# Softmax reciprocals repeated through DRAM, value products copied out by ScalarE and scaled later by GpSimd

## The chip, the cores and the metric

The kernel runs on one core of a Trainium2 chip. The metric is the device time of one execution in microseconds (us), lower being better. The core has five engines that run their own instruction queues and wait for one another by semaphores: TensorE (PE in the profile; its weight loads are shown as PEld), VectorE (DVE), ScalarE (ACT), GpSimd (POOL) and SyncE (SP), which here only issues DMA transfers. TensorE writes its results into PSUM, the other engines work on PSUM and SBUF.

## The reference

Causal attention with a decay, for 4 batches of 8 heads, 576 positions and 64 columns a head, and behind it two feed-forward layers (512 to 2048 to 512) over the 2304 tokens. What the change touches is the last step of the attention:

```python
scores = scores - np.max(scores, axis=-1, keepdims=True)
attn = np.exp(scores)
attn = attn / (np.sum(attn, axis=-1, keepdims=True) + 1e-09)
return np.matmul(attn, v).astype(np.float32)
...
h = x @ w_in                       # first layer; x is the attention's output
g = h * np.clip(h + 3.0, 0.0, 6.0) / 6.0
x = g @ w_out
h = x @ w_in2                      # second layer
return (np.maximum(h, 0.0) + alpha * np.minimum(h, 0.0)) @ w_out2
```

The kernel doesn't divide the scores' exponentials; it multiplies by the values first and scales the product by the reciprocal of the row's sum.

## The kernel before

Attention works on 16 pairs of heads (4 batches of 4 pairs). A pair is cut into nine units: four blocks of 128 query rows of the first head (positions 0 to 3), the last 64 rows of both heads together (position 4), four blocks of the second head (positions 5 to 8). One loop counts units, and in each step the instructions of several units are written in an order fixed by the string ORD = "TMEVDS": T transposes the exponentials of the unit five steps back (L396, L400, TensorE), M takes row maxima of the unit one step back (L340, VectorE), E does the exponentials of the unit two steps back (L348, ScalarE, with the row sums), V copies the transposed tile out of PSUM (L407, L412 and L413; ScalarE, every fourth block VectorE), D runs the steps that were put off to this time, S does the scores of the step's own unit (L363 to L380, TensorE). No scheduler reorders them: each engine runs its instructions in this order.

The steps put off belong to a pair whose last unit is U. At U + 3 (RD) `recips` forms ten reciprocals a row on VectorE and has GpSimd repeat them 64 times into rw (L93, called at L425). At U + 6 (SD) `spread` has TensorE transpose rw (four transposes tr at L435, one tj at L438), and ScalarE copies the result into rcb: one reciprocal for each column of the output, repeated over the 64 partitions of a head (L436, L440 twice). At U + 7 (PA) and U + 9 (PB) `stage3` forms the value products of output columns 0 to 255 and 256 to 575 (L453), both in the one PSUM buffer pv, and VectorE multiplies pv by rcb into the token array R (L460). U + 6 is position 5 of the next pair, U + 7 position 6, U + 9 position 8. Below, the two products are called the first and the second product of a pair; pairs are counted from 0.

R holds the tokens in three blocks of 768, so that the 576 tokens of batches 1 and 2 lie over a border (`x_places`), and their pieces are cut there.

In the same steps the heads of the next pair are prepared: `prep_head` (positions 3 and 7; GpSimd, L93 for q and k), two steps later `prep_low` (L331 on GpSimd, L332 on VectorE) and `copy_k` (a DMA from SBUF to SBUF, L325). SyncE issues all of these transfers in the order of the program: the head's rows (L295 rqk), the values (L300), the constant rows (L312, L313), copy_k. Conversions of the feed-forward weights and of the first tokens are laid between units by tables (CONV_ATT and others; lines 138 to 187 and 240 to 248), on ScalarE, VectorE and GpSimd.

Buffers: three PSUM buffers of tag tp, which the transposes of the exponentials share with tr and tj; one buffer for pv; four for the scores; one for rcb.

From position 147 on the steps of the feed-forward layers begin (DRAIN), and behind the attention they run alone to the end.

Of the kernel before, what the change touches and what calls it, by code (L numbers as in the profile page):

```python
# [21 lines left out]
def decay_attention_ffn2_kernel(ctx, tc, qk, v, f, wi1, wo1, wi2, wo2, alpha, out):  # L22
# [20 lines left out]
    LM, LE, LT, LV = 1, 2, 5, 5  # L43
    RD, SD, PA, PB = 3, 6, 7, 9
    DRAIN = {9 * NP + 3: 2, 9 * NP + 4: 2, 9 * NP + 6: 2, 9 * NP + 7: 2}
# [36 lines left out]

    f_d = [dram.tile([128, 4, KH * 256], F32, name=f"fd{g}") for g in range(NC)]
    aq_d = dram.tile([2, 32, 4, QW], F32, name="aq_d")
    ak_d = dram.tile([2, 32, 4, S], F32, name="ak_d")
# [192 lines left out]
    def attention():  # L278
        with ExitStack() as ax:
# [135 lines left out]
            def recips(p):  # L415

                ss = sm.pop(p)
                rc = st.tile([128, 10], F32, tag="rc", name="rc")
                nc.vector.tensor_scalar(out=ss[:, 4:5], in0=ss[:, 4:5], scalar1=ss[:, 9:10], scalar2=None,
                                        op0=ALU.add)  # L420
                nc.vector.tensor_copy(out=ss[:, 9:10], in_=ss[:, 4:5])
                nc.vector.tensor_scalar(out=rc, in0=ss, scalar1=1e-9, scalar2=None, op0=ALU.add)
                nc.vector.reciprocal(out=rc, in_=rc)
                rw = rcp.tile([128, KT, 2, 64], F32, tag="rw", name="rw")
                scaled(  # L425
                    "P", rw, rc.rearrange("p (a i) -> p i a", a=2).unsqueeze(3).broadcast_to([128, KT, 2, 64]))
                rcs[p] = rw

            def spread(p):

                rw = rcs.pop(p)
                t = rcp.tile([128, S], F32, tag="rcb", name="rcb")
                tr = ps_pt.tile([128, 4, 128], F32, tag="tp", name="tr")
                for i in range(4):
                    nc.tensor.transpose(tr[:, i, :], rw[:, i].rearrange("p a b -> p (a b)"), ident)  # L435
                nc.scalar.copy(out=t[:, 0:512], in_=tr.rearrange("p a b -> p (a b)"))  # L436
                tj = ps_pt.tile([128, 4, 128], F32, tag="tp", name="tj")
                nc.tensor.transpose(tj[:, 0, :], rw[:, 4].rearrange("p a b -> p (a b)"), ident)  # L438
                for a in range(2):
                    nc.scalar.copy(out=t[64 * a:64 * a + 64, 512:S], in_=tj[64 * a:64 * a + 64, 0, 64 * a:64 * a + 64])  # L440
                rcb[p] = t

            def stage3(p, part):
# [5 lines left out]
                for j in js:  # L449
                    lo = max(q0, 128 * j)  # L450
                    kk = min(128, S - 128 * j)
                    for a in range(2):
# [3 lines left out]
                            rhs=pts[2 * p + a][0:kk, j * PR + lo:j * PR + q1],  # L456
                            start=(j == js[0]), stop=(j == js[-1]))
                for view, t0, t1 in x_places(hp, b * S + q0, b * S + q1):
                    c0, c1 = t0 - b * S, t1 - b * S
                    nc.vector.tensor_mul(out=view, in0=pv[:, c0 - q0:c1 - q0], in1=rcb[p][:, c0:c1])  # L460
                if part == 1:
                    for d, key in ((vs, p), (rcb, p), (pts, 2 * p), (pts, 2 * p + 1)):
                        d.pop(key)

# [97 lines left out]
            for k, (a, h) in enumerate(zip(("", "l0", "l1", "l2", "a3", "a4", "a6", "l3", "l4", "a5", "l6", "l5"),  # L562
                                           ("0", "1", "2", "", "", "", "3", "4", "6", "", "5", ""))):
                for c in range(KH):
                    if a:
                        aside(places[k], {"l": lows, "a": adds}[a[0]][int(a[1]), c])
                    if h:
                        aside(places[k], highs[int(h), c])
            for t in range(len(units) + max(LV, PB) + 1):
                now = todo.pop(t, [])  # L570
# [12 lines left out]
                if t < len(units):  # L583
                    p, ab, i = units[t]
                    pos = t % 9
                    if ab == 1 and i == 3:
                        for d, fn in ((RD, lambda p=p: recips(p)), (SD, lambda p=p: spread(p)),
                                      (PA, lambda p=p: stage3(p, 0)), (PB, lambda p=p: stage3(p, 1))):
                            todo.setdefault(t + d, []).append(fn)
# [324 lines left out]
```

## Time and profile before

| | us |
|---|---|
| median of 3 runs (982.57 to 983.43) | 982.98 |
| the profiled execution | 982.49 |
| its span | 980.7 |
| TensorE busy | 955.6 (97%) |
| VectorE busy | 705.7 (72%) |
| GpSimd busy | 594.4 (61%) |
| ScalarE busy | 539.7 (55%) |

The profiled execution lies 0.49 us under the median and 1.79 us over its own span. Busy shares are averages over two stages with different limits: attention, about 0 to 222 us, and the layers behind it, in which TensorE is busy in nearly every slice. In the timelines a row's length is that of one instruction from its start to its end, and neighbours overlap a little, so the distance from one start to the next is shorter than a length.

### The profile page before, as it was taken

How to read it: one execution, taken by the hardware profiler on the slowest of the kernel's cores; microseconds unless marked ns; L12 is line 12 of the kernel's file. 1: busy time of each engine (PE TensorE's matmuls, PEld its weight loads, DVE VectorE, ACT ScalarE, POOL GpSimd, SP SyncE). 2: the span in 40 equal slices, each digit the busy share in tenths (PEclk: the TensorE clock that was granted, in tenths of full speed). 3: DMA queues.
4: the chain of work that ended last, by engine and by line, in shares of the span. 5: the costliest groups of instructions: out<-in, count | busy, mean ns of one | idle time of the engine just before them, and what ended most of it. 6: DMA issues, size and time to landing. Idle time of an engine off the chain costs nothing.

```text
span 980.7 us, 15789 instructions
## 1 busy us (share of the span) xinstructions
PE 955.6 (97%) x5488; PEld 860.4 (88%) x5488; DVE 705.7 (72%) x1274; ACT 539.7 (55%) x1348; POOL 594.4 (61%) x583
## 2 busy tenths in 40 slices
PE   5999999999999999999999999999999999999998
PEld 4767766678999999999999999899898988898897
DVE  7898979956697777876788666347897778625454
ACT  5678877777555554555564456644454546343231
POOL 7567589956646665578476379565646668422231
PEclk9999999999999999999999999999999999999999
DMA  7646576501414443410468732413434410253541
GB/s 211 201 136 213 181 250 196 144 35 43 161 65 182 183 183 108 160 59 9 166 246 312 272 130 108 161 65 140 173 118 182 182 65 17 103 204 139 216 161 64
DMA packets 36195, 145.79 MB, mean 149 GB/s; under 512 B 4860, under 2 KB 4860, under 8 KB 33012
## 3 DMA queue, kind: packets, MB, share of 16 engines
q1 hardware_dynamic: 36112, 144.79, 42.0%
q8 instruction: 43, 0.70, 0.3%
q14 instruction: 36, 0.29, 0.1%
q10 hardware_dynamic: 4, 0.00, 0.0%
HBM read 97.21 MB, written 43.42 MB: 143 GB/s over the span
## 4 chain that ended last, share of the span: by engine, by line
PE 85%; DVE 8%; issue 2%; POOL 2%; ACT 1%; SPq 1%; DMA 1%; POOLq 0%; DVEq 0%; ACTq 0%
PE o L744 20%; PE hA L704 20%; PE o L742 19%; PE hC L704 10%; PE hB L704 5%; PE pv L453 4%; DVE nm L340 2%; PE tp L396 2%; PE sc L363 2%; DVE q L332 1%; PE sc L364 1%; DVE pt L407 1%; POOL g L687 1%; DMA k<-ak_d 1%; PE sc L375 0%
## 5 line engine op out<-in xcount | busy, mean ns | idle before, releaser
L687 POOL TENSOR_TENSOR g<-t,g 128x384 fp32r<-128x384 f32 x192 | 205.6, 1071 | 287.6 <-ACT g L686 270.4
L742 PE MATMUL o<-g,wo 128*128 128x384 f32 x1152 | 232.2, 340 | 1.8 <-POOL wo L187 1.1
L704 PE MATMUL hA<-xh,wi 128*128 128x384 f32 x768 | 224.3, 338 | 1.1 <-DVE hD L718 0.7
L744 PE MATMUL o<-wo,g 128*128 128x512 f32 x864 | 223.2, 394 | 0.0
L742 PEld LDWEIGHTS o<-g,wo 128*128 128x128 f32 x1152 | 205.0, 189 | 3.2 <-POOL wo L187 1.4
L686 ACT CAST g<-t 128x384 fp32r<-128x384 f32 x192 | 98.6, 514 | 176.8 <-DVE t L681 91.8
L744 PEld LDWEIGHTS o<-wo,g 128*128 128x128 f32 x864 | 160.6, 188 | 25.8
L762 DVE TENSOR_TENSOR r<-o,r 128x512 f32<-128x512 f32 x126 | 86.7, 688 | 86.2 <-PE o L744 85.7
L704 PEld LDWEIGHTS hA<-xh,wi 128*128 128x128 f32 x768 | 141.5, 188 | 4.7 <-DVE hD L718 1.0
L704 PE MATMUL hA<-xl,wi 128*128 128x384 f32 x384 | 129.5, 337 | 0.0
L751 DVE SCALAR_TENSOR_TENSOR r<-o,r 128x384 f32<-128x384 f32 x168 | 92.1, 552 | 49.1 <-PE o L742 48.3
L704 PE MATMUL hC<-xh,wi 128*128 128x384 f32 x384 | 114.4, 338 | 0.0
L348 ACT ACTIVATE p<-sc,nm 128x128 f32<-128x128 f32 (+4 forms) x160 | 84.2, 530 | 16.6 <-DVE nm L340 14.5
L340 DVE TENSOR_REDUCE nm<-sc 128x1 f32<-128x128 f32 (+4 forms) x160 | 71.6, 469 | 6.1 <-PE sc L365 4.0
L704 PEld LDWEIGHTS hA<-xl,wi 128*128 128x128 f32 x384 | 72.1, 188 | 3.2
L704 PEld LDWEIGHTS hC<-xh,wi 128*128 128x128 f32 x384 | 71.3, 189 | 2.1 <-issue 0.2
L248 POOL TENSOR_TENSOR xl<-r,xh 128x384 fp32r<-128x384 f32 x59 | 69.7, 1197 | 3.3 <-ACT xh L243 2.8
L396 PE MATMUL tp<-ident,p 128*128 128x128 f32 x384 | 68.6, 282 | 1.0 <-ACT pt L412 0.6
L363 PE MATMUL sc<-k,q 128*128 128x256 f32 (+2 forms) x128 | 55.0, 429 | 12.2 <-DVE k L331 8.8
L709 ACT COPY s<-hA 128x384 f32<-128x384 f32 x96 | 45.8, 477 | 35.1 <-PE hA L704 34.9
L704 PE MATMUL hC<-xl,wi 128*128 128x384 f32 x192 | 65.0, 338 | 0.0
L704 PE MATMUL hB<-xh,wi 128*128 128x384 f32 x192 | 57.1, 338 | 0.0
(133 smaller groups left out, 1725.6 us busy)
## 6 DMA issues: line engine op xcount, KB each, us to landing
wid<-wi SPq DMA_DIRECT2D x24, 896.0 KB
wi<-wid SPq DMA_DIRECT2D x12, 1792.0 KB
rqk<-in_qk SPq DMA_DIRECT2D x32, 608.0 KB
raw<-in_wi SPq DMA_DIRECT2D x32, 512.0 KB
raw<-in_wo SPq DMA_DIRECT2D x32, 512.0 KB
wod<-wo SPq DMA_DIRECT2D x24, 512.0 KB
wo<-wod SPq DMA_DIRECT2D x12, 1024.0 KB
vt<-in_v SPq DMA_DIRECT2D x16, 320.0 KB
```

The costliest lines, as they stand in the source:

```text
L248: e.tensor_sub(out=XS[k][1][:, b, c], in0=x, in1=XS[k][0][:, b, c].bitcast(F32))
L340: nc.vector.tensor_reduce(out=nm[:, i:i + 1], in_=src, axis=AX.X, op=ALU.max, negate=True)
L348: nc.scalar.activation(out=pt[:, c0:c0 + cw], in_=src, func=AF.Exp, bias=nm[:, 0:1], scale=1.0, accum_out=dsts[i])
L363: nc.tensor.matmul(out=sc[:, 0:n], lhsT=q1[:, qs], rhs=k1[:, 0:n], start=True, stop=False)
L396: nc.tensor.transpose(tp[:, j, :], pt[:, 128 * j:128 * j + 128], ident)
L686: nc.scalar.copy(out=gt[n][i][:, 0], in_=hold["g"])
L687: nc.gpsimd.tensor_sub(out=gt[n][i][:, 1], in0=hold["g"], in1=gt[n][i][:, 0].bitcast(F32))
L704: nc.tensor.matmul(out=h, lhsT=a, rhs=b[:, x, kc], start=new and kc + e == 0, stop=kc == KH - 1 and e == 2, skip_group_check=not new)
L742: nc.tensor.matmul(out=o[:, 0:NB], lhsT=a[:, cs], rhs=b, start=st, stop=sp)
L744: nc.tensor.matmul(out=o, lhsT=b[:, cs], rhs=a, start=st, stop=sp)
L751: later(0, lambda: nc.vector.scalar_tensor_tensor(out=acc, in0=o[:, 0:NB], scalar=1.0 / 6.0, in1=acc, op0=ALU.mult, op1=ALU.add))
L762: nc.vector.tensor_add(out=acc, in0=o, in1=acc)
```

## The change

`recips` no longer has GpSimd repeat the reciprocals. `spread` transposes the 128 x 10 tile rc once; ScalarE copies the 10 x 128 result to SBUF, and SyncE stores it in DRAM (rc_d). `widen`, two steps later (U + 8), has SyncE read it back in three transfers that repeat a row over 64 partitions, into rcb. `stage3` only forms the products. `settle`, one step behind each product (U + 8 and U + 10), has ScalarE copy pv into R unscaled, and `normalize` (U + 12, PN) has GpSimd multiply R in place by rcb.

```diff
--- before.py
+++ after.py
@@ -41,7 +41,7 @@
     TAIL = S - 512
     PR = S - 128
     LM, LE, LT, LV = 1, 2, 5, 5
-    RD, SD, PA, PB = 3, 6, 7, 9
+    RD, SD, PA, PB, PN = 3, 6, 7, 9, 12
     DRAIN = {9 * NP + 3: 2, 9 * NP + 4: 2, 9 * NP + 6: 2, 9 * NP + 7: 2}
     CONV_ATT = "m0 22 f0 23 s0 24 j0 25 g0 26 m1 31 f1 32 s1 33 j1 34 g1 35 hb 37 lb 39 S1 42 S3 42 S2 45 S4 45 ha 51 la 54 hc 53 lc 60 hd 60 ld 63 m2 69 f2 70 s2 71 j2 72 g2 73 m3 78 f3 79 s3 80 j3 81 g3 83 ho0 78 lo0 87 ho1 87 lo1 91 wi0 90 wi1 93 wo0 99 wo1 102 r0 54 r1 63 r2 93 r3 104"
     CONV_ATT1 = "r0 131 r1 141 m0 108 f0 109 s0 110 j0 114 g0 115 m1 117 f1 118 s1 119 j1 123 g1 124 S1 143 S3 145 S2 146 ha 146 hc 146 hb 147 la 147 lc 147 lb 148 S4 149 hd 149 ld 150 m2 150 f2 151 s2 151 j2 152 g2 153"
@@ -81,6 +81,7 @@
     wo_d = [[dram.tile([128, 2, FT * DM], F32, name=f"wod{ff}{g}") for g in range(NG)] for ff in range(2)]
 
     f_d = [dram.tile([128, 4, KH * 256], F32, name=f"fd{g}") for g in range(NC)]
+    rc_d = [dram.tile([2, KT * 128], F32, name=f"rc{i}") for i in range(NP)]
     aq_d = dram.tile([2, 32, 4, QW], F32, name="aq_d")
     ak_d = dram.tile([2, 32, 4, S], F32, name="ak_d")
 
@@ -421,24 +422,31 @@
                 nc.vector.tensor_copy(out=ss[:, 9:10], in_=ss[:, 4:5])
                 nc.vector.tensor_scalar(out=rc, in0=ss, scalar1=1e-9, scalar2=None, op0=ALU.add)
                 nc.vector.reciprocal(out=rc, in_=rc)
-                rw = rcp.tile([128, KT, 2, 64], F32, tag="rw", name="rw")
-                scaled(
-                    "P", rw, rc.rearrange("p (a i) -> p i a", a=2).unsqueeze(3).broadcast_to([128, KT, 2, 64]))
-                rcs[p] = rw
+                rcs[p] = rc
 
             def spread(p):
 
-                rw = rcs.pop(p)
+                rc = rcs.pop(p)
+                tr = ps_pt.tile([128, 4, 128], F32, tag="tp", name="tr")
+                nc.tensor.transpose(tr[0:2 * KT, 0, :], rc, ident)
+                flat = rcp.tile([2 * KT, 128], F32, tag="rw", name="rw")
+                nc.scalar.copy(out=flat, in_=tr[0:2 * KT, 0, :])
+                nc.sync.dma_start(out=rc_d[p].rearrange("a (i c) -> (a i) c", c=128), in_=flat)
+
+            def widen(p):
+
                 t = rcp.tile([128, S], F32, tag="rcb", name="rcb")
-                tr = ps_pt.tile([128, 4, 128], F32, tag="tp", name="tr")
-                for i in range(4):
-                    nc.tensor.transpose(tr[:, i, :], rw[:, i].rearrange("p a b -> p (a b)"), ident)
-                nc.scalar.copy(out=t[:, 0:512], in_=tr.rearrange("p a b -> p (a b)"))
-                tj = ps_pt.tile([128, 4, 128], F32, tag="tp", name="tj")
-                nc.tensor.transpose(tj[:, 0, :], rw[:, 4].rearrange("p a b -> p (a b)"), ident)
-                for a in range(2):
-                    nc.scalar.copy(out=t[64 * a:64 * a + 64, 512:S], in_=tj[64 * a:64 * a + 64, 0, 64 * a:64 * a + 64])
+                for a, c0, w in ((0, 0, S), (1, 0, 512), (1, 512, TAIL)):
+                    s0 = c0 + TAIL * (c0 > 0)
+                    nc.sync.dma_start(out=t[64 * a:64 * a + 64, c0:c0 + w],
+                                      in_=rc_d[p][a, s0:s0 + w].unsqueeze(0).broadcast_to([64, w]))
                 rcb[p] = t
+
+            def normalize(p):
+                b, hp = divmod(p, NPAIR)
+                t = rcb.pop(p)
+                for view, t0, t1 in x_places(hp, b * S, b * S + S):
+                    nc.gpsimd.tensor_mul(out=view, in0=view, in1=t[:, t0 - b * S:t1 - b * S])
 
             def stage3(p, part):
                 b, hp = divmod(p, NPAIR)
@@ -455,12 +463,18 @@
                             lhsT=vt[0:kk, j, 64 * a:64 * a + 64],
                             rhs=pts[2 * p + a][0:kk, j * PR + lo:j * PR + q1],
                             start=(j == js[0]), stop=(j == js[-1]))
+                if part == 1:
+                    for d, key in ((vs, p), (pts, 2 * p), (pts, 2 * p + 1)):
+                        d.pop(key)
+                pvs[p, part] = pv
+
+            def settle(p, part):
+                b, hp = divmod(p, NPAIR)
+                pv = pvs.pop((p, part))
+                q0, q1 = ((0, 256), (256, S))[part]
                 for view, t0, t1 in x_places(hp, b * S + q0, b * S + q1):
-                    c0, c1 = t0 - b * S, t1 - b * S
-                    nc.vector.tensor_mul(out=view, in0=pv[:, c0 - q0:c1 - q0], in1=rcb[p][:, c0:c1])
-                if part == 1:
-                    for d, key in ((vs, p), (rcb, p), (pts, 2 * p), (pts, 2 * p + 1)):
-                        d.pop(key)
+                    c0, c1 = t0 - b * S - q0, t1 - b * S - q0
+                    nc.scalar.copy(out=view, in_=pv[:, c0:c1])
 
 
             NPP = 64
@@ -566,7 +580,8 @@
                         aside(places[k], {"l": lows, "a": adds}[a[0]][int(a[1]), c])
                     if h:
                         aside(places[k], highs[int(h), c])
-            for t in range(len(units) + max(LV, PB) + 1):
+            pvs = {}
+            for t in range(len(units) + max(LV, PN) + 1):
                 now = todo.pop(t, [])
                 for ch in ORD:
                     if ch == "D":
@@ -585,7 +600,9 @@
                     pos = t % 9
                     if ab == 1 and i == 3:
                         for d, fn in ((RD, lambda p=p: recips(p)), (SD, lambda p=p: spread(p)),
-                                      (PA, lambda p=p: stage3(p, 0)), (PB, lambda p=p: stage3(p, 1))):
+                                      (PA, lambda p=p: stage3(p, 0)), (PA + 1, lambda p=p: settle(p, 0)),
+                                      (SD + 2, lambda p=p: widen(p)), (PB, lambda p=p: stage3(p, 1)),
+                                      (PB + 1, lambda p=p: settle(p, 1)), (PN, lambda p=p: normalize(p))):
                             todo.setdefault(t + d, []).append(fn)
                     if pos == 2:
                         load_v(p)
```

Three places show how the queues change; L numbers are those of each kernel.

ScalarE, before: the stretch between the copies into rcb of a pair (L436, L440) and the exponentials that follow the second copy of three transposed blocks (L407 with 128x3x128).

```order
L436 COPY rcb<-tr 128x512 [waits PE_49]
L440 COPY rcb<-tj 64x64 [waits PE_49]
L440 COPY rcb<-tj 64x64
L348 ACTIVATE p,sm<-sc,nm 128x288 [waits DVE_49,Activation_49]
L348 ACTIVATE p,sm<-sc,nm 128x288
L407 COPY pt<-tp 128x2x128 [waits PE_49]
L138 ACTIVATE wc<-raw 128x512 [waits DMAHW0_49,Pool_49]
L348 ACTIVATE p,sm<-sc,nm 128x128 [waits DVE_49,Activation_49]
L407 COPY pt<-tp 128x3x128 [waits PE_49]
L348 ACTIVATE p,sm<-sc,nm 128x256 [waits DVE_49,Activation_49]
L348 ACTIVATE p,sm<-sc,nm 128x384 [waits DVE_49,PE_49,Activation_49]
```

The same stretch now. L433 is the copy of the transposed reciprocals, L477 the copy of the first product, here in two pieces because a border of R lies in it.

```order
L433 COPY rw<-tr 10x128 [waits DMAHW1_49,PE_49]
L349 ACTIVATE p,sm<-sc,nm 128x288 [waits DVE_49,Activation_49]
L349 ACTIVATE p,sm<-sc,nm 128x288
L408 COPY pt<-tp 128x2x128 [waits PE_49]
L139 ACTIVATE wc<-raw 128x512 [waits DMAHW4_49,Pool_49]
L349 ACTIVATE p,sm<-sc,nm 128x128 [waits DVE_49,Activation_49]
L408 COPY pt<-tp 128x3x128 [waits PE_49]
L477 COPY r_80<-pv 128x192
L477 COPY r_81<-pv 128x64
L349 ACTIVATE p,sm<-sc,nm 128x256 [waits DVE_49,Activation_49]
L349 ACTIVATE p,sm<-sc,nm 128x384 [waits DVE_49,PE_49,Activation_49]
```

Three copies at the head are one, and two copies of the product stand behind the copy of three transposed blocks and in front of the next exponentials.

TensorE, before: the transposes and scores ahead of the second product of the same pair (L453 with 64x320).

```order
L396 MATMUL tp<-ident,p 128x128 x2
L363 MATMUL sc<-k_1334,q_1332 128x384 [waits Activation_49]
L364 MATMUL sc<-k_1335,q_1333 128x384
L365 LDWEIGHTS identb
L365 MATMUL sc<-maskb,identb 128x128
L396 MATMUL tp<-ident,p 128x128 [waits PE_49]
L396 MATMUL tp<-ident,p 128x128 x3
L453 MATMUL pv<-pt,vt 64x320 [waits DVE_49,PE_49]
L453 MATMUL pv<-pt,vt 64x320 x5
```

The same place now, where the product is at L461.

```order
L397 MATMUL tp<-ident,p 128x128 x2
L364 MATMUL sc<-k_1334,q_1332 128x384 [waits Activation_49]
L365 MATMUL sc<-k_1335,q_1333 128x384
L366 LDWEIGHTS identb
L366 MATMUL sc<-maskb,identb 128x128
L397 MATMUL tp<-ident,p 128x128 x4
L461 MATMUL pv<-pt,vt 64x320 [waits PE_49,Activation_49]
L461 MATMUL pv<-pt,vt 64x320 x5
```

The first matmul of the second product waited for VectorE's multiplication of the first one; it now waits for ScalarE's copy.

SyncE, before: the transfers from one copy_k (L325) to the next.

```order
L325 DMA k_1444<-k_1443 64x576 [waits DMAHW5_49,Pool_49]
L312 DMA q_1536<-aq_d 4x640 [waits DMAHW6_49,PE_49]
L313 DMA k_1538<-ak_d 4x576 [waits DMAHW7_49]
L295 DMA rqk<-in_qk 128x1216 [waits DMAHW0_49,DVE_49]
L325 DMA k_1538<-k_1537 64x576 [waits DMAHW1_49,Pool_49]
```

The same stretch now: L434 stores the reciprocals, L441 reads them back.

```order
L434 DMA rc_123<-rw 10x128 [waits DMAHW1_49,Activation_49]
L326 DMA k_1444<-k_1443 64x576 [waits DMAHW2_49,Pool_49]
L441 DMA rcb<-rc_123 64x576 [waits DMAHW3_49,DMAHW1_49]
L441 DMA rcb<-rc_123 64x512 [waits DMAHW4_49]
L441 DMA rcb<-rc_123 64x64 [waits DMAHW5_49]
L313 DMA q_1534<-aq_d 4x640 [waits DMAHW6_49,PE_49]
L314 DMA k_1536<-ak_d 4x576 [waits DMAHW7_49]
L296 DMA rqk<-in_qk 128x1216 [waits DMAHW0_49,DVE_49]
L326 DMA k_1536<-k_1535 64x576 [waits Pool_49]
```

A store that waits for ScalarE stands in front of the first copy_k, and three reads, the first of which waits for the store to have landed, in front of the head's transfers and the second copy_k.

## Rows read from the trace of the kernel before

**Rows 1.** Windows view, two stretches: length, busy us (instructions) by engine, PEclk, DMA share, GB/s.

```profile
140.00:176.00 36.00, 33.61 (x257) 23.88 (x254) 31.16 (x67) 27.08 (x99) 31.91 (x32) 1.00 0.70 210
...
176.00:208.00 32.00, 30.32 (x234) 20.97 (x232) 26.49 (x54) 24.35 (x92) 25.11 (x24) 1.00 0.38 114
```

**Rows 2.** Timeline of TensorE, 91 to 104 us: start, length, engine, line, operation, operands, count.

```profile
91.76 2.42 PE L453 MATMUL pv<-pt,vt 128*64 128x320 f32 x20
...
99.52 0.60 PE L435 MATMUL tr<-ident,rw 128*128 128x128 f32 x4
...
99.98 0.37 PE L363 MATMUL sc<-k,q 128*128 128x256 f32 x1
...
103.20 1.03 PE L453 MATMUL pv<-pt,vt 128*64 128x320 f32 x6
```

**Rows 3.** Timeline of ScalarE, 95 to 104 us, same columns, idle before in brackets.

```profile
95.39 0.37 ACT L412 COPY pt<-tp 128x256 f32<-128x256 f32 x1 [2.35 <-PE tp L396]
...
100.15 0.59 ACT L436 COPY rcb<-tr 128x512 f32<-128x512 f32 x1
...
101.09 0.50 ACT L348 ACTIVATE p<-sc,nm 128x288 f32<-128x288 f32 x1
...
103.23 0.50 ACT L407 COPY pt<-tp 128x384 f32<-128x384 f32 x1
```

**Rows 4.** Timelines of TensorE and ScalarE around the second product of pairs 1 and 14.

```profile
43.37 1.03 PE L453 MATMUL pv<-pt,vt 128*64 128x320 f32 x6
...
43.44 0.47 ACT L407 COPY pt<-tp 128x384 f32<-128x384 f32 x1
...
203.57 0.76 PE L453 MATMUL pv<-pt,vt 128*64 128x320 f32 x4
...
203.02 0.49 ACT L407 COPY pt<-tp 128x384 f32<-128x384 f32 x1
```

**Rows 5.** Waits view, 29 to 208 us: waiter, releaser, us in total, times, longest.

```profile
ACT pt L412 <- PE tp L396: 25.6, 14, 2.6
...
DVE r L460 <- PE pv L453: 15.5, 11, 1.7
...
ACT p L348 <- DVE nm L340: 12.4, 23, 1.4
```

**Rows 6.** Groups by shape, 0 to 222 us: count, busy us, mean ns, idle before.

```profile
L460 DVE TENSOR_TENSOR r<-pv,rcb 128x256 f32<-128x256 f32 x12 | 4.9, 409 | 3.2 <-ACT rcb L436 2.3 <-ACT p L348 0.8
...
L460 DVE TENSOR_TENSOR r<-pv,rcb 128x320 f32<-128x320 f32 x12 | 5.8, 486 | 10.7 <-PE pv L453 10.7
...
L407 ACT COPY pt<-tp 128x256 f32<-128x256 f32 x32 | 11.8, 369 | 0.0
...
L436 ACT COPY rcb<-tr 128x512 f32<-128x512 f32 x16 | 9.6, 599 | 0.6 <-PE tr L435 0.3
...
L93 POOL TENSOR_SCALAR rw<-rc 128x640 f32<-128x640 f32 x16 | 11.9, 742 | 45.7 <-DVE rc L423 26.8 <-PE tp L396 16.0 <-PE sc L377 2.1
...
L331 POOL TENSOR_TENSOR k<-rqk,k 64x576 fp32r<-64x576 f32 x31 | 44.9, 1448 | 2.6
```

**Rows 7.** Timelines of VectorE and GpSimd, 107 to 115 us.

```profile
107.01 0.81 DVE L332 SCALAR_TENSOR_TENSOR q<-rqk,q 64x640 fp32r<-64x640 f32 x1
...
112.90 1.91 DVE L332 SCALAR_TENSOR_TENSOR q<-rqk,q 64x640 fp32r<-64x640 f32 x1
...
112.72 1.40 POOL L331 TENSOR_TENSOR k<-rqk,k 64x576 fp32r<-64x576 f32 x1
```

**Rows 8.** Timelines of VectorE and GpSimd, 97 to 98 us.

```profile
97.53 0.22 DVE L423 RECIPROCAL rc<-rc 128x10 f32<-128x10 f32 x1
...
97.90 0.73 POOL L93 TENSOR_SCALAR rw<-rc 128x640 f32<-128x640 f32 x1 [2.43 <-DVE rc L423]
```

**Rows 9.** Timelines of SyncE and TensorE, 182 to 187 us.

```profile
182.22 0.47 SPq L325 DMA_DIRECT2D k<-k  x1
...
186.75 0.29 PE L377 MATMUL sc<-k,q 68*128 68x288 f32 x1
```

## The prediction

> **What bounds the kernel now.** I read the windows view by stages first. Everything that changes lies in the attention, the first 222 us; behind it TensorE is full, so a microsecond won or lost in the attention is one at the end. In the attention four engines are loaded at once: between 140 and 176 us TensorE is busy 33.6 of 36 us, VectorE 31.2, GpSimd 31.9, ScalarE 27.1 [rows 1]. A share doesn't say who sets the pace, so I went to the timelines of one ordinary pair. TensorE starts the second product of pair 5 at 91.76 and that of pair 6 at 103.20, 11.44 us later [rows 2]. ScalarE stands idle for 2.35 us while the second product runs, since nothing new is transposed meanwhile, and resumes at 95.39 [rows 3]. The waits view shows that this is its usual wait: 25.6 us over 14 pairs, against 12.4 us in 23 waits for VectorE's maxima [rows 5]. From 95.39 on ScalarE works with hardly a gap until its copy of three transposed blocks, 103.23 to 103.73, which ends 0.53 us after the second product has started [rows 2, 3]. The reader is to see that ScalarE, the least busy of the four, runs about half a microsecond behind TensorE at this point, and that this is free now, because the second product waits for VectorE's multiplication alone. VectorE in turn waits 15.5 us in 11 waits for products to end [rows 5].
>
> **The change part by part.** All sums are made against the profiled execution's 982.49 us, which lies 0.49 us under the median of the runs.
>
> TensorE. Five transposes a pair (tr, tj) take 0.46 us from 99.52 to the next scores at 99.98 [rows 2]; four of five go, about 0.37 us a pair, 5.9 us in 16. That is gained only where TensorE sets the pace.
>
> ScalarE. Three copies into rcb go: 100.15 to 101.09, 0.94 us [rows 3]. Three come. A copy of 256 columns takes 0.37 us and one of 512 takes 0.60 [rows 6], so by their slope the 320 columns of the second settle are about 0.43 and the 128 of the transposed reciprocals about 0.26; less the overlap of neighbours, some 0.1 each, these two are 0.50. The first settle is the third: 0.37 less overlap, about 0.30 (with the cut at a border, 0.4). In total ScalarE is left about 0.15 us a pair lighter. What counts is where the copies stand.
>
> The new wait. The first settle stands behind the copy of three transposed blocks, and the second product waits for it, because pv is one buffer. Over pairs 1 to 14 that block copy ends on average 0.35 us after the second product's present start: 0.54 at pair 1 (43.44 + 0.47 against 43.37), 0.06 before it at pair 14; these are the first and the last of the 14 [rows 4]. ScalarE's work ahead of it shrinks by 0.94 - 0.50 = 0.44. Then comes the settle, 0.30, and the hand-over. The hand-over from ScalarE to TensorE has no row of its own; from VectorE's reciprocal (97.53 + 0.22) to GpSimd's start at 97.90 it is 0.15 us [rows 8]. The bounds are 0 and twice that, and I take 0.15. The second product so starts 0.35 - 0.44 + 0.30 + 0.15 = 0.36 us later a pair, and each later start delays the transposes for which ScalarE waits next, so it adds up: 14 x 0.36 = 5.0 us. With the bounds of the hand-over it is 2.9 to 7.1. Queued behind the waiting product on TensorE are the scores of position 8 and the next transposes; ScalarE and VectorE both wait for those.
>
> VectorE. Two multiplications go, 0.41 and 0.49 us a pair [rows 6]. The second stood mostly in a wait for TensorE (10.7 us before the 12 of 320 columns). What this frees comes back only where ScalarE waits for maxima: at most the 12.4 us of rows 5, at least nothing. Part of those waits lies in the stretch in which ScalarE would wait for TensorE anyway (the longest, 1.4 us, does), so I take a third: -4.0 us.
>
> GpSimd. The repetition, 0.74 us [rows 6], goes; the scaling in place comes, two inputs in SBUF over 576 columns and 128 partitions. Its nearest row is L331, 64 partitions and 576 columns, 1.45 us [rows 6]. I take 1.4 for one piece and 1.65 for the two pieces of batches 1 and 2, so 0.7 to 0.9 us more a pair. GpSimd stood idle 45.7 us in front of the 16 repetitions [rows 6], so in most pairs this is hidden. Between 140 and 208 us it is not quite: 4.1 and 6.9 us idle [rows 1] over about five pairs. There I charge two pairs, +1.5 us (bounds 0 and 5 x 0.9 = 4.5). What is queued behind a late scaling are the head's q and k, then copy_k, then TensorE's scores.
>
> SyncE and the transfers. Per pair one store and three reads come. The store waits for ScalarE; behind it stands copy_k. The first read waits for the store to land; behind it stand the other reads, the constant rows, the next head and the second copy_k. How long a small store takes to land is in no row. A copy_k issued at 182.22 is read by the matmul at 186.75 without a wait [rows 9], so 144 KB land within 4.5 us; the store has 5 KB. The second copy_k is used eight positions after the transposed reciprocals, 8/9 of 11.44 us or 10.2 us; two landings and seven issues of up to 0.47 us [rows 9] fit if a landing takes up to 3.5 us. If it took 4.5, TensorE would stall 2 us a pair wherever the queues are that full. I take nothing, since the store is the smaller; for the range I keep four such pairs around the weight stores, 8 us.
>
> [...]
>
> Sum: 5.0 - 4.0 + 1.5 = +2.5 us, 985.0 us.
>
> **The rivals.**
> *VectorE's relief wins* (faster). Besides the multiplications, GpSimd loses its wait for the reciprocals (2.43 us idle at 97.90 [rows 8]), so L331 may run ahead of L332 instead of beside it, which frees up to 1.1 us of VectorE a pair [rows 7]. If most of the 12.4 us go, ScalarE catches up, the new wait isn't met, and TensorE's own path decides: 982.5 less 5.9, or half of it where another engine holds on. About 978. Against it: ScalarE is nearly gapless in the ordinary pair, so there is little for VectorE to give back.
> *Everything is hidden.* The new wait falls into time that ScalarE gains by its own lighter load, and what TensorE saves is waited off: 983.0. For it: the terms are tenths of a microsecond; against it: they add up over 14 pairs.
> *GpSimd becomes the bound* (slower). From pair 9 on, with the first tokens' conversions on it, each scaling is paid in full, 0.7 to 0.9 us over six pairs, about 5 us, partly as blocked L332 and conversions on VectorE. It decides once a scaling ends after the next head's q would have started. On top of the forecast that is 990. For it: 31.9 of 36 us [rows 1]; against it: 45.7 us of idle time ahead of the repetitions.
>
> **How the numbers follow.** The forecast has 0.42, its own range is 981.5 to 989 (relief 1 to 7.5 us). Relief wins has 0.27, all hidden 0.15, GpSimd 0.16. A measurement of this kernel tells about 0.2%, 2 us, from no change. Faster by more is the relief case, 0.27. Within 2 us are the hidden case and some two fifths of the forecast's own range, 0.32. Slower is the rest, 0.41. The range, 976 to 992, runs from the full 5.9 us of TensorE to the GpSimd case and the late transfers of a few pairs.
>
> **What would show it.** Right: a wait of the second product's first matmul (L461) for ScalarE's copy (L477) in most pairs, half a microsecond or more; VectorE's 15.5 us of waits for products gone; ScalarE's wait at the copies after the second product unchanged or longer; distance between second products 11.8 us or so in an ordinary pair. Wrong: second products that start without a wait and closer together than 11.4 us (relief); TensorE's scores waiting for the transfers of L326, or GpSimd's q waiting for rows (late transfers); GpSimd without idle time from 140 us on and VectorE's L332 longer in the mean than now (GpSimd).

## The result, and the profile after

The changed kernel takes 994.67 us (median of 4 runs, 992.71 to 995.83), the kernel before on the same chip 983.09: ratio 1.0126, 95% interval 1.0114 to 1.0137. It is slower, by 11.6 us between the medians and 12.4 us by the ratio, and outside the range forecast. The profiled execution took 994.84 us, with a span of 993.1.

The loss lies in the attention. From the timelines of TensorE, start of the second product (L461) after the change less before (L453), us:

```
pair    1     3     5     6     7     8     9    10    11    13    15
     -0.85 -0.18  0.16  1.41  3.82  5.22  5.09 12.19 12.89 12.57 13.02
```

Up to pair 5 next to nothing is lost: the lead of pair 1 goes at 0.25 us a pair. Then 5 us go in pairs 6 to 8 and 7.1 from pair 9 to pair 10; the forecast had a steady 0.36 a pair. Windows view after, the stretches of [rows 1]:

```profile
140.00:176.00 36.00, 29.20 (x207) 20.62 (x207) 20.76 (x47) 22.26 (x86) 28.39 (x29) 0.91 0.71 235
176.00:208.00 32.00, 28.17 (x220) 19.61 (x218) 24.26 (x51) 23.61 (x88) 29.70 (x29) 1.00 0.62 179
```

In the first stretch no engine is fuller than before; in the second GpSimd is (29.7 us for 25.1). In the first TensorE falls from 33.6 to 29.2 us of 36, and its granted clock, 1.00 in [rows 1], is 0.91. TensorE's timeline after shows where:

```profile
104.61 2.42 PE L461 MATMUL pv<-pt,vt 128*64 128x320 f32 x20 [0.54 <-ACT r L477]
...
113.61 0.37 PE L378 MATMUL sc<-k,q 68*128 68x288 f32 x1 [1.78 <-DMA k<-k]
```

```profile
145.47 2.42 PE L461 MATMUL pv<-pt,vt 128*64 128x320 f32 x20 [0.40 <-ACT r L477]
...
152.88 0.39 PE L376 MATMUL sc<-k,q 128*128 128x288 f32 x1
...
158.13 0.58 PE L378 MATMUL sc<-k,q 68*128 68x288 f32 x1 [4.58 <-DMA k<-k]
158.50 0.48 PE L376 MATMUL sc<-k,q 128*128 128x288 f32 x1
```

Twice TensorE waits long for copy_k's rows, 1.78 and 4.58 us. Before, the waits view of the attention has no wait of TensorE for copy_k; [rows 9] is one place without it. SyncE's timeline after shows why the rows of the second wait were late:

```profile
138.95 0.62 SPq L193 DMA_DIRECT2D wid<-wi  x1
...
142.43 0.29 SPq L434 DMA_DIRECT2D rc<-rw  x1
142.82 0.48 SPq L326 DMA_DIRECT2D k<-k  x1
149.45 1.75 SPq L441 DMA_DIRECT2D rcb<-rc  x3
...
152.16 0.51 SPq L296 DMA_DIRECT2D rqk<-in_qk  x1
152.71 0.48 SPq L326 DMA_DIRECT2D k<-k  x1
```

The store leaves at 142.43, behind a weight store (wid). The first read waits for it to land and leaves at 149.45, 7.0 us after a store of 5 KB. The reads take 1.75 us to issue, the head's rows follow, and the second copy_k leaves only at 152.71. The chain of waits says how long these transfers took (start, length):

```profile
101.40 3.65 DMA rc<-rw
...
108.22 5.25 DMA k<-k
...
152.71 5.32 DMA k<-k
```

Behind these two waits TensorE runs slower for a while. Windows view after, behind the two waits (PEclk is the third number from the end):

```profile
116.00:120.00 4.00, 4.00 (x25) 2.75 (x23) 3.02 (x6) 3.56 (x14) 2.83 (x4) 0.65 0.41 116
...
156.00:160.00 4.00, 1.87 (x9) 1.68 (x9) 0.64 (x2) 0.00 (x0) 2.41 (x3) 0.55 1.04 339
160.00:164.00 4.00, 4.00 (x23) 2.64 (x21) 1.83 (x5) 2.31 (x10) 3.92 (x5) 0.60 0.87 307
```

TensorE's granted clock is 1.00 from 152 to 156 us, 0.50 from 158 to 163 and 1.00 again from 164; the 288 columns of L376 take 0.48 us at 158.50 against 0.39 at 152.88. The cost of the lower clock is an estimate from these rows, the ungranted share of the busy time: 0.45 x 1.87 + 0.40 x 4.00 = 2.4 us. This and the 4.58 us of waiting are 7.0 of the 7.1 us lost there. In pairs 6 to 8 the 1.78 us of waiting and, by the same estimate, 0.35 x 4.00 = 1.4 us at the lower clock are 3.2 of the 5 us; the rest is spread over waits of up to 1.1 us for ScalarE and VectorE.

The waits view after, 29 to 208 us, answers to [rows 5]:

```profile
DVE nm L341 <- PE sc L366: 38.7, 24, 3.4
ACT pt L413 <- PE tp L397: 33.2, 14, 2.7
...
ACT p L349 <- DVE nm L341: 8.2, 15, 1.4
...
PE sc L378 <- DMA k<-k: 7.0, 3, 4.6
PE pv L461 <- ACT r L477: 6.9, 12, 1.0
```

The forecast wait of the second product for ScalarE is there, 6.9 us in 12. ScalarE waits 33.2 us at the copies behind the second product against 25.6, and VectorE, relieved of the products, stands 38.7 us before TensorE's scores. Its 15.5 us of waits for products are gone, and ScalarE's waits for maxima fell from 12.4 to 8.2 us. ScalarE's timeline around pair 5, as [rows 3]:

```profile
91.40 0.47 ACT L477 COPY r<-pv 128x192 f32<-128x192 f32 x2
...
95.57 0.37 ACT L413 COPY pt<-tp 128x256 f32<-128x256 f32 x1 [2.67 <-PE tp L397]
...
96.30 0.44 ACT L477 COPY r<-pv 128x320 f32<-128x320 f32 x1
```

Groups of the attention after (0 to 235 us), as [rows 6]:

```profile
L333 DVE SCALAR_TENSOR_TENSOR q<-rqk,q 64x640 fp32r<-64x640 f32 x32 | 32.6, 1017 | 0.7 <-POOL q L94 0.4 <-ACT q L90 0.2
...
L449 POOL TENSOR_TENSOR r<-r,rcb 128x576 f32<-128x576 f32 x7 | 9.9, 1417 | 18.8 <-ACT r L477 18.0 <-DMA rqk<-in_qk 0.8
...
L423 DVE TENSOR_SCALAR rc<-sm 128x10 f32<-128x10 f32 x16 | 8.5, 530 | 5.2 <-ACT p L349 4.1
...
L477 ACT COPY r<-pv 128x320 f32<-128x320 f32 x12 | 5.2, 437 | 0.0
L477 ACT COPY r<-pv 128x256 f32<-128x256 f32 x12 | 4.6, 385 | 0.0
```

The operations were costed well: the scaling takes 1.42 us (1.4 estimated), the settles 0.39 and 0.44 (0.37 and 0.43). Two groups of the kernel before (0 to 222 us) are the counterparts of L333 and L423:

```profile
L332 DVE SCALAR_TENSOR_TENSOR q<-rqk,q 64x640 fp32r<-64x640 f32 x32 | 42.4, 1326 | 2.0 <-POOL q L93 1.9
...
L422 DVE TENSOR_SCALAR rc<-sm 128x10 f32<-128x10 f32 x16 | 5.0, 314 | 3.5 <-ACT p L348 2.2
```

L333 has become shorter, 1017 for 1326 ns, and L423 longer, 530 for 314.

### The profile page after: what moved, and what is told of

Same layout as the page of the kernel before. It is cut to its first block, busy times and chain, and to the rows that moved or that the text cites. A ratio compares the mean times of both kernels' runs of the same rounds, so it can differ in the third digit from the quotient of the medians.

```text
span 993.1 us, 15800 instructions
## 1 busy us (share of the span) xinstructions
PE 952.5 (96%) x5424; PEld 855.2 (86%) x5424; DVE 686.1 (69%) x1234; ACT 537.6 (54%) x1356; POOL 603.1 (61%) x591
## 4 chain that ended last, share of the span: by engine, by line
PE 81%; DVE 6%; ACT 4%; DMA 3%; issue 2%; POOL 2%; SPq 1%; DVEq 0%; ACTq 0%; POOLq 0%
PE o L761 20%; PE hA L721 19%; PE o L759 19%; PE hC L721 10%; PE hB L721 5%; PE pv L461 4%; DVE nm L341 2%; ACT p L349 2%; DMA k<-k 2%; PE tp L397 1%; PE sc L364 1%; PE sc L365 1%; ACT pt L408 1%; DMA rc<-rw 1%; ACT r L477 1%
## 5 line engine op out<-in xcount | busy, mean ns | idle before, releaser
L349 ACT ACTIVATE p<-sc,nm 128x128 f32<-128x128 f32 (+4 forms) x160 | 84.4, 532 | 16.3 <-DVE nm L341 10.2
L249 POOL TENSOR_TENSOR xl<-r,xh 128x384 fp32r<-128x384 f32 x59 | 67.6, 1161 | 3.3 <-ACT xh L244 2.8
L461 PE MATMUL pv<-pt,vt 128*64 128x320 f32 (+4 forms) x448 | 54.0, 374 | 7.8 <-ACT r L477 7.8
```

What stands on the lines that cost most here:

```text
L249: e.tensor_sub(out=XS[k][1][:, b, c], in0=x, in1=XS[k][0][:, b, c].bitcast(F32))
L349: nc.scalar.activation(out=pt[:, c0:c0 + cw], in_=src, func=AF.Exp, bias=nm[:, 0:1], scale=1.0, accum_out=dsts[i])
L461: nc.tensor.matmul(out=pv[64 * a:64 * a + 64, lo - q0:q1 - q0], lhsT=vt[0:kk, j, 64 * a:64 * a + 64], rhs=pts[2 * p + a][0:kk, j * PR + lo ...
```

## The experiments

Theories. A: the transfers (SyncE's queue, the landing, the bytes). B: the second product's wait for ScalarE's copy. C: GpSimd's scaling in SBUF. Ratios are to the kernel before in the same runs, with 95% intervals; a thousandth is 0.98 us.

**e3, the transfers alone:** the kernel before, plus a 5 KB store of rcb and three small reads of 48, 40 and 8 columns in the changed kernel's places of SyncE, used by nothing.

```diff
+ nc.sync.dma_start(out=<rc_d[p]>, in_=<5 KB of rcb>)     # at U + 6
+ three reads of 48, 40 and 8 columns of rc_d[p]          # at U + 8
```

> The kernel before, with a store of 5 KB at the place of the changed kernel's store and three small reads of it (64 partitions, 48, 40 and 8 columns) at the place of its reads; nobody uses what they bring. Theory A: 988 to 993 us, TensorE waits for k<-k, though the reads move hardly any bytes. Theories B and C: 982 to 984, as before.

Measured: 1.0119 (1.0104 to 1.0135). Waits view (29 to 230 us) and SyncE's timeline:

```profile
PE sc L378 <- DMA k<-k: 7.5, 4, 5.1
```

```profile
141.72 0.29 SPq L443 DMA_DIRECT2D rc<-rcb  x1
142.11 0.80 SPq L326 DMA_DIRECT2D k<-k  x1
149.08 1.75 SPq L449 DMA_DIRECT2D spare<-rc  x3
```

Nearly the same places lose the time, 3.6 us from pair 4 to 6 and 7.9 from pair 9 to 10, with VectorE's multiplication and everything else as before. The store, the wait for its landing and three reads of 24 KB in all are enough to cost the whole 12 us. The bytes of the wide reads are not needed for that.

**e4, no wait for the landing:** the reads take rows of the constants (aq_d), so the output is scaled by other numbers.

```diff
- in_=rc_d[p][a, s0:s0 + w]...
+ in_=aq_d[a, 0, 0:1, s0:s0 + w]...
```

> The changed kernel, whose three reads take a row that was written at the start instead of this pair's reciprocals (so the scaling uses wrong factors): same transfers, same bytes, same order, but no read waits for the store. Theory A, if the wait for the landing does it: 985 to 989 us. Theory A, if it is the bytes and the order alone: 991 to 995. Theories B and C: 992 to 996.

Measured: 1.0075 (1.0060 to 1.0090). The landing is worth 5.0 us here, not the 12 of e3. Waits view (29 to 230 us):

```profile
PE pv L461 <- ACT r L477: 10.2, 16, 1.6
...
PE sc L378 <- DMA k<-k: 0.3, 1, 0.3
```

With k on time, the wait for ScalarE grows to all 16 pairs, from 7.3 us in 13 of the changed kernel in the same window.

**e8, the store on ScalarE's queue:** `nc.sync.dma_start` becomes `nc.scalar.dma_start` for the store.

> The changed kernel with the store of the reciprocals issued by ScalarE, behind its own copy, instead of SyncE; the reads stay with SyncE at U + 8. Theory A1 (the 5 KB wait in SyncE's queue behind the bulk transfers that were issued ahead of them): on a queue of its own the store lands within 3 us of its issue, the first read no longer waits 5.3 us on average (17.8 us in 14 waits), and the time falls to 987 to 990, near the 989.0 without any wait. Theory A2 (the store waits for the shared transfer engines, whatever its queue): the waits stay and the time is 993 to 996.

Measured: 1.0174 (1.0145 to 1.0203). ScalarE's copy for the store in pair 9, and SyncE's first reads behind it:

```profile
143.94 0.25 ACT L433 COPY rw<-tr 10x128 f32<-10x128 f32 x1
```

```profile
149.36 1.74 SPq L441 DMA_DIRECT2D rcb<-rc  x3
```

From the copy's end to the reads it is 5.2 us, on a queue that up to 240 us carries 0.09 of the 43.73 MB moved: the store is late whatever its queue, and A1, by which it lands within 3 us, falls. (The 5.3 us of the expectation are the longest wait, not the average: 17.8 us in 14 waits are 1.3 each.) Why the kernel became slower still, beyond A2's 993 to 996, is open. In both kernels SyncE had issued a weight store ahead of it (138.95 us in the changed kernel, 140.75 here), and the small one landed late from either queue, 7.0 and 5.2 us. What held it back is not shown.

**e1, the reads later:** behind the second copy_k, the scaling three steps later.

```diff
- RD, SD, PA, PB, PN = 3, 6, 7, 9, 12
+ RD, SD, PA, PB, PN = 3, 6, 7, 9, 15
- (SD + 2, lambda p=p: widen(p))
+ (SD + 5, lambda p=p: widen(p))
```

> The changed kernel with its three reads of the reciprocals issued three steps later (step U + 11 instead of U + 8, so behind the second copy_k of the pair), and the scaling three steps later (U + 15). Theory A (SyncE: copy_k and the next head stand behind reads that wait for the store to land, and TensorE waits for k): TensorE's 7.0 us of waits for k<-k go and the time falls to 984 to 988 us, the rest being the wait of the second product for ScalarE. Theory B (the second product's wait for ScalarE is the loss): no change, 992 to 996. Theory C (GpSimd's scaling in SBUF slows VectorE and GpSimd): no change, 992 to 996.

Measured: 1.0142 (1.0110 to 1.0173), a miss for A as stated. The waits for k are gone, and as much is lost elsewhere. One place, VectorE, GpSimd and the window behind it:

```profile
112.81 0.88 DVE L423 TENSOR_SCALAR rc<-sm 128x10 f32<-128x10 f32 x1
```

```profile
112.05 1.61 POOL L449 TENSOR_TENSOR r<-r,rcb 128x192 f32<-128x192 f32 x2 [0.52 <-ACT pt L408]
```

```profile
116.00:120.00 4.00, 4.00 (x20) 2.56 (x20) 2.44 (x6) 3.39 (x12) 2.95 (x3) 0.50 0.49 109
```

An addition on ten columns takes 0.88 us beside the scaling, against 0.31 in the mean before, and the two conversions ahead of it take 1.20 and 0.94 us, against 0.68 each before. The maxima behind them are late, TensorE runs short, and its clock is down to 0.50 for four microseconds.

**e2, e5, e6, without DRAM:** before's repetition and transposes; e2 with ScalarE's copies and the scaling at U + 12, e5 with VectorE's copies in place of its multiplications, e6 like e2 without the scaling (the output is not divided).

```diff
e2:  before + settle on ScalarE (U + 8, U + 10) + normalize on GpSimd (U + 12)
e5:  e2 with nc.vector.tensor_copy, in the steps U + 7 and U + 9
e6:  e2 without normalize
```

> The changed kernel without the way through DRAM: reciprocals repeated by GpSimd and transposed five times by TensorE as before; ScalarE copies the products and GpSimd scales them as in the changed kernel. Theory A: 984 to 988 us, no wait of TensorE for k. Theory B: 991 to 996. Theory C: 992 to 997, since GpSimd has the repetition as well as the scaling.

> The kernel without the way through DRAM (the repetition by GpSimd and five transposes as before, the scaling on GpSimd in SBUF at U + 12), but VectorE copies the products out in the steps in which it multiplied them before, so that TensorE's second product waits for VectorE as in the kernel before. Before is 981.5 on this chip. Theory B (the new wait of the second product for ScalarE's copy is what cost 15 us without DRAM): 981 to 985, and the waits of L459 for ScalarE are gone. Theory C (GpSimd's scaling in SBUF costs, by blocking VectorE's L332 or by GpSimd's own delay): 990 to 997, as with ScalarE's copies. Mixed: 985 to 990.

> The kernel without the way through DRAM, ScalarE copying the products out one step later, and the scaling on GpSimd left out (the output isn't divided by the row sums; everything else is issued as in that kernel). Theory B: 991 to 997, as with the scaling (996.4), with the second product's waits for ScalarE still about 25 us over 16 pairs. Theory C: 981 to 986, with those waits far shorter.

Measured: e2 1.0153 (1.0138 to 1.0168), e5 1.0064 (1.0049 to 1.0079), e6 1.0099 (1.0084 to 1.0114). e2 fits B as well as C. With no extra transfer at all B, less what VectorE is spared, costs 9.7 us (e6), and C 6.3 (e5). Part of e5 can't be in the changed kernel, as this wait shows: GpSimd's scaling stands ahead of the next pair's repetition, and TensorE waits for that.

```profile
PEld tr L435 <- POOL rw L93: 5.7, 7, 1.4
...
PE tr L435 <- POOL rw L93: 4.3, 5, 1.2
```

**e7, e9, e10, e11, the ladder** (outputs are not the scaled product): e7 is e4 with VectorE's copies. e9 is e7 with the reads cut to 48, 40 and 8 columns and R multiplied by itself; e10 the same with ScalarE's copies; e11 is e9 without the scaling.

> The changed kernel with reads that take rows of the constants' table instead of the stored reciprocals, so that no read waits for a landing (the output is scaled by other numbers; 989.0 with ScalarE's copies), and with VectorE copying the products out in the steps in which it multiplied before. TensorE has four transposes a pair less than the kernel before, ScalarE three copies less. Theory B: 976 to 982, at or below before. Theory C: 986 to 991. If TensorE's transposes and ScalarE's copies are worth something on the path, it lies under 981.5 by B.

> The kernel with reads that wait for no landing and VectorE's copies (989.6), but the three reads are cut to 48, 40 and 8 columns, a twelfth of the bytes, and GpSimd multiplies R by itself in place of the repeated reciprocals (same shapes, two inputs in SBUF; the output is not the scaled product). Theory bytes (the 288 KB that the reads bring make the head's rows and copy_k late, GpSimd then waits for rqk and everything behind shifts): 979 to 983, GpSimd's 18.6 us of waits for rqk fall below 8. Theory C (GpSimd's scaling blocks VectorE or makes GpSimd late): 986 to 991.

> The same narrow reads and scaling, with ScalarE's copies one step after the product, as in the changed kernel. Theory B (the wait for ScalarE's copy costs on its own): 986 to 991, 6 to 9 us above the narrow kernel with VectorE's copies. Theory bytes: 981 to 984, close to the narrow kernel with VectorE's copies, and the 989.0 of the kernel with wide reads was the bytes.

> The narrow kernel with VectorE's copies and without the scaling (the output is the unscaled product). What is left of the change is what it removes: four transposes, three copies of ScalarE and GpSimd's repetition per pair, for one copy, one store and three small reads. If TensorE sets the pace in the attention: 975 to 979 (the 5.9 us of its transposes). If it does not: 979 to 983. Theory C: at least 3 us below the narrow kernel with the scaling; otherwise within 2 us of it.

Measured, each row with one thing more than the one above it:

| | ratio (interval) | us to before | step |
|---|---|---|---|
| e11: what the change removes, with small transfers that wait for no landing | 0.9963 (0.9948, 0.9979) | -3.6 | |
| e9: + scaling on GpSimd | 1.0005 (0.9987, 1.0022) | +0.5 | +4.1 |
| e10: + copies by ScalarE | 1.0045 (1.0028, 1.0063) | +4.4 | +3.9 |
| e4: + 288 KB of reads a pair | 1.0075 (1.0060, 1.0090) | +7.4 | +2.9 |
| changed: + wait for the landing | 1.0126 (1.0114, 1.0137) | +12.4 | +5.0 |

A step is uncertain by some 2 us, and its size depends on its place: with the wide reads, VectorE's copies bring nothing (e7, 1.0091, against e4's 1.0075). Two steps hold more than their name says. ScalarE's copies also spare VectorE its own. And in e4 the scaling waits for its reads, 5.4 us in 3 waits, which R multiplied by itself does not. How the wide reads cost their 2.9 us is not shown: GpSimd's waits for the head's rows, which were to fall below 8 us with the bytes, are 18.8 us in e9 and 18.6 in e7.

Pair 10 is a sensitive place even where no read waits for a landing. The profiled execution of e11, the slowest of its ten (975.19 to 983.07 us), loses 7.35 us from pair 9 to pair 10 as well. There copy_k itself is late; it was issued behind two weight stores, and TensorE waits for it until 8.8 us after its issue:

```profile
134.08 0.90 SPq L326 DMA_DIRECT2D k<-k  x1
```

```profile
142.90 0.38 PE L365 MATMUL sc<-k,q 68*128 68x256 f32 x1 [2.98 <-DMA k<-k]
```

So a late landing beside the weight stores can cost this much without the new store's wait, which is one way to it and in the changed kernel the one that was met.

**e12, both new waits off the path:** VectorE's copies, reads at U + 11, scaling at U + 14.

> The whole computation again: the changed kernel with VectorE's copies in the steps in which it multiplied before, the reads at U + 11 behind the second copy_k, and the scaling at U + 14, a step in which neither VectorE's L333 nor the reciprocals' additions are issued. Both waits that the change brought, for ScalarE's copy and for the store's landing, are so off the path. If nothing else costs: 981 to 984. Theory bytes: 986 to 991, with GpSimd waiting for rqk. Theory C: 986 to 991, with GpSimd nearly without idle time.

Measured: 1.0089 (1.0063 to 1.0114), 991.2 us where nothing else costing meant 981 to 984. Up to pair 6 it gains, 4.2 us; pairs 7 and 8 lose 9.6. There VectorE's conversions of weights, and GpSimd beside them:

```profile
105.11 1.90 DVE L150 SCALAR_TENSOR_TENSOR wc<-raw,wc 128x512 uint32<-128x512 uint32 x1
...
107.13 1.00 DVE L155 SCALAR_TENSOR_TENSOR wc<-raw,wc 128x512 uint32<-128x512 uint32 x1
```

```profile
104.60 1.86 POOL L332 TENSOR_TENSOR k<-rqk,k 64x576 fp32r<-64x576 f32 x1
...
107.56 1.10 POOL L94 TENSOR_SCALAR k<-rqk 128x576 fp32r<-128x576 f32 x1
```

In the kernel before, the same two (L149 and L154) stand where GpSimd waits for the reciprocals:

```profile
107.75 0.68 DVE L149 SCALAR_TENSOR_TENSOR wc<-raw,wc 128x512 uint32<-128x512 uint32 x1
...
108.55 0.68 DVE L154 SCALAR_TENSOR_TENSOR wc<-raw,wc 128x512 uint32<-128x512 uint32 x1
```

```profile
110.58 0.73 POOL L93 TENSOR_SCALAR rw<-rc 128x640 f32<-128x640 f32 x1 [5.67 <-DVE rc L423]
```

**e13, e14, e15, the hold.** Theory F: GpSimd's wait for the reciprocals had kept its work apart from VectorE's conversions. GpSimd copies the ten reciprocals where it repeated them before, in e12, in e9 and in the changed kernel.

```diff
+ rg = rcp.tile([128, 2 * KT], F32, tag="rg", name="rg")
+ nc.gpsimd.tensor_copy(out=rg, in_=rc)
- rcs[p] = rc
+ rcs[p] = rg
```

> The kernel with VectorE's copies and late reads (991.2), with one instruction more: GpSimd copies the 128 x 10 reciprocals in the step in which it repeated them before, and TensorE transposes this copy. GpSimd's order is so tied to VectorE's reciprocals again, as in the kernel before. Theory F (GpSimd, freed from its wait for the reciprocals, runs its SBUF work beside VectorE's conversions, L150 and L155, which take 1.9 and 1.0 us there instead of 0.68 each, and the 9.6 us lost at pairs 7 and 8 follow from it): 980 to 985, with L150 and L155 near 0.7 us again and a granted clock of 1.0 between 103 and 140 us. Theory scaling (GpSimd's own 1.65 us a pair make it late): 989 to 994.

> The same hold in the kernel with narrow reads that wait for no landing, VectorE's copies and the scaling of R by itself (982.8; 977.9 without the scaling). Theory F: 977 to 981, most of the scaling's 4.8 us were the missing hold. Theory scaling: 982 to 985.

> The changed kernel with the hold alone (994.7 without it). Theory F on top of the others: 990 to 993. If the landing of the store, ScalarE's copies and the reads' bytes hold it anyway: 993 to 997.

Measured: e13 1.0103 (1.0082 to 1.0123), e14 0.9996 (0.9987 to 1.0006), e15 1.0148 (1.0122 to 1.0175). As a cause of the totals F falls: e13 was to take 980 to 985 us and took 992.4, and e14's gain on e9, 0.9 us by the ratios, is within the uncertainty. In its own place it holds in part: in e13 pairs 7 and 8 lose 2.6 us instead of 9.6, the clock is 1.00 from 103 to 140 us, and the second two conversions, 1.14 and 1.84 us in e12, are short (the first L150, beside late rows of the head, still takes 1.89):

```profile
122.54 0.68 DVE L150 SCALAR_TENSOR_TENSOR wb<-raw,wb 128x512 uint32<-128x512 uint32 x1
...
124.50 0.63 DVE L155 SCALAR_TENSOR_TENSOR wb<-raw,wb 128x512 uint32<-128x512 uint32 x1
```

As much was lost later, 3.5 us of it from pair 9 to 10. Of e12's 8.9 us at the end of the span 3.1 stand at the last second product; behind it GpSimd waits (e12, 217 to 245 us):

```profile
POOL r L449 <- DMA rcb<-rc: 5.9, 1, 5.9
```

**e16, e17, e18, the last pair early:** its reads at U + 8 and its scaling at U + 12; e16 from e12, e17 from e13, e18 with the hold in pairs 6 and 7 only.

```diff
- (SD + 5, lambda p=p: widen(p))
+ (SD + (2 if p == NP - 1 else 5), lambda p=p: widen(p))
- (PN, lambda p=p: normalize(p))
+ (PN - 2 * (p == NP - 1), lambda p=p: normalize(p))
```

> The kernel with VectorE's copies, reads at U + 11 and scaling at U + 14 (991.2; its span is 8.9 us over before, of which 3.1 stand at the last second product and 5.8 come behind it, where GpSimd waits 5.9 us for the last pair's reads), with the last pair's reads at U + 8 and its scaling at U + 12. If the late last scaling is what the 5.8 us are: 984 to 987. If the handover to the layers loses them anyway: 989 to 993.

> The same with GpSimd's copy of the reciprocals in every pair (992.4 with the late last pair, 5.0 at the last second product and 6 behind it). If the late last scaling is the cause: 985 to 989, no better than without the hold. Otherwise 990 to 994.

> The same with GpSimd's copy of the reciprocals in pairs 6 and 7 alone, beside whose next pairs VectorE's conversions stand. If the hold is worth something where the conversions are, and costs only where they are not (TensorE's waits for k at 98 and 107 us with the hold in all pairs): 980 to 984. If not: 984 to 989, as without.

Measured: e16 1.0036 (1.0013 to 1.0059), 5.2 us better than e12, as expected of the late last pair; e17 1.0070 (1.0045 to 1.0095); e18 1.0021 (1.0002 to 1.0040), the best version with the change, still not faster than before at the median. It lies between its two expected ranges and 1.5 us from e16, so what the hold is worth in pairs 6 and 7 is not shown. No version of the whole computation beats it.

## Why the prediction was wrong

The direction was right, the size (+2.5 for +11.6 us between the medians) wrong. The step that failed is the one on SyncE and the transfers: "I take nothing, since the store is the smaller". Measured: +5.0 for the landing and +2.9 for the wide reads on top of the rest, and +11.7 for the transfers alone (e3). Three things in it were wrong. The landing of a small store was bounded by one copy_k [rows 9] (DMA share 0.67 from 182.2 to 186.75 us) and taken as less for its fewer bytes, but the 5 KB took 3.65 us in pair 6 (share 0.60 from 101 to 105 us) and 7.0 behind a weight store (0.99 from 142 to 146 us), and copy_k itself up to 8.8 beside such stores (e11). The chain from the store to the second copy_k's landing was allowed 10.2 us and took 15.6 (142.43 to 158.03). And a wait of TensorE was priced at its own length, while the lower clock behind it added an estimated 2.4 us to the 4.58 and 1.4 to the 1.78. The bytes of the reads themselves, as many as two copy_k a pair, were not charged at all.

The new wait for ScalarE: right in its mechanism. 0.54 and 0.40 us stand in front of the second products shown, and their starts move by 0.25 us a pair up to pair 5, forecast 0.36. Its size was not measured alone. From e9 to e10 the wait comes and VectorE's relief with it: +3.9 measured, where the two terms together had 5.0 - 4.0 = +1.0.

TensorE's transposes and VectorE's relief: 0 and -4.0 taken. e11 shows -3.6 for all that is removed, with VectorE's copies as long as its multiplications were. So it comes without those multiplications going, and that it lies near the -4.0 is luck; TensorE's, ScalarE's and GpSimd's shares in it were not separated. In the changed kernel VectorE's relief came as idle time in front of TensorE's scores (38.7 us). ScalarE's waits for maxima did fall by the third that was taken, 12.4 to 8.2 us, but those behind the second product rose by more, 25.6 to 33.2; that the relief won anything is not shown.

The scaling: +1.5 taken, +4.1 measured, inside the bounds of 0 to 4.5. GpSimd's part of the relief rival came true: VectorE's L333 overlaps GpSimd's L332 in 11 of 32 instances, before their counterparts in 19 (mean 1017 for 1326 ns). The same freedom put GpSimd's work beside VectorE's conversions (in e12 1.84 us for 0.63 with the hold of e13; in the changed kernel 1.08 and 1.29 us for 0.68 behind pair 6, though its twelve conversions of this kind up to 200 us are shorter in sum, 10.7 us for 12.3) and beside its addition of ten columns (530 for 314 ns).

Which lengths go with such neighbours, up to 240 us: before, L332 took 0.81 us in each of its 7 instances with no GpSimd work beside it and 1.61 in the mean of the 19 beside L331, and the conversions of L149 and L154 0.68 in the mean of 7 without such work and 1.21 in that of 9 with some. After the change the addition of ten columns (L423) took 0.17 us in its 3 instances without and 0.22 to 0.95 in the 13 with some; before (L422), 5 of 16 had some. Why the lengths go together is not shown.

Without the two transfer terms the sum is -3.6 + 4.1 + 3.9 = +4.4 us (e10), near the forecast of +2.5, but in part by terms that were off in opposite directions. The forecast's own range has a slip, too: with a relief of 1 us its sum is 988.0, not 989. What is not settled is how the terms add in general: e6 has B at 9.7 us where the ladder has 3.9.

## What to carry to other kernels

Cost a small transfer by its place in the issuing queue: what was issued ahead of it, which instruction waits for it to land, and what is issued behind that; take its landing from the stretch in which it is to land (here 7.0 us for 5 KB behind a weight store, 3.65 in pair 6), and let what it delays reach TensorE. Where TensorE is full, look at its granted clock behind each longer wait, too (here, by the estimate above, 2.4 us more behind 4.58 us and 1.4 behind 1.78). An engine's wait can be what keeps its work apart in time from another's (two conversions on VectorE took 1.14 and 1.84 us in e12, 0.68 and 0.63 in e13, in which GpSimd waits for the reciprocals again), so ask what it does sooner when its wait is removed.

## What was not expected of the hardware

Behind the wait of 4.58 us TensorE's granted clock was 0.50 from 158 to 163 us, and behind that of 1.78 us 0.50 from 116 to 118, while it was 1.00 behind waits of 1.06 and 0.98 us at 128 and 133 us; in e1 gaps of 0.51 and 0.82 us close together were followed by 0.50 from 116 to 120 us. Kernels with the change spread more from run to run: e18 ran from 977.83 to 986.69 us and e16 from 979.17 to 991.0 in 10 runs each, the kernel before from 980.78 to 982.97 in 19. In e16 the mean granted clock goes with the time, 1.000 in the fastest run and 0.988 in the slowest. What sets the clock of a run is not shown. A store of 5 KB took 7.0 us to land beside weight stores, and 5.2 us there from another queue; a copy of 144 KB took 8.8 us there in e11.
